# Transformer block: fill matmuls in column-tiled form beside the attention, and layer-norm transposes on TensorE

## The chip, the cores and the metric

One core of one Trainium2 chip. The metric is the device time in microseconds of one execution of the whole kernel. The kernel before was run three times: 1266.35, 1267.56 and 1269.32 us, median 1267.56.

The engines are called by their names in the profile: PE (TensorE matmul), PEld (its weight loads), DVE (VectorE), ACT (ScalarE), POOL (GpSimd), SP (the queue that issues the DMAs). PE computes `lhsT.T @ rhs`: lhsT is loaded as weights, rhs streams through, and the result lies in one of eight PSUM banks of 128 x 512 f32.

## The reference

A pre-norm transformer block in bf16 on one sequence of S = 2048 tokens, D = 1024, 32 heads of 32, a feed-forward width of F = 3584.

```
qkv = layernorm(x) @ wqkv                     # per head: q, k, v of 32 columns
p   = softmax(q @ k.T * 32**-0.5)             # 2048 x 2048 for each of 32 heads
h   = x + concat(p @ v) @ wo
out = h + gelu(layernorm(h) @ w1 + b1) @ w2 + b2
```

## The kernel before

**Planner.** The kernel is written down by a small planner in Python. Every operation is handed to `plan.task` with the buffers that it reads and writes and a cost in ns; the planner keeps for each engine the time at which it is free by these costs, works out the semaphore waits, and the order in which operations are recorded is the order in which each engine runs them. The chip knows nothing of the costs; they only decide the order. `pe` (L277) records a matmul, of kind F (128x128), R (32x128, a quarter of the rows) or C (128x32, a quarter of the columns); where the kind changes it books 105 ns more.

**Prologue (to about 69 us).** Sixteen tiles of 128 tokens of x are loaded, normalized (DVE statistics L456 to L458, POOL and DVE for the reciprocal root, ACT subtracts the mean L693, DVE scales L696) and transposed into `xnT`, since all projections need the model dimension on the partitions. Tiles 0 to 5 (`TP = 6`) are transposed on PE, eight 128x128 blocks a tile (L499), and evicted by ACT (L710). Tiles 6 to 15 are transposed by ten DMAs that SP issues (`ln1_t`, L714). A list of candidates with priorities (L732 to L763) interleaves these with the key projection of the first group of four heads for all four blocks of tokens (`proj_k`, L552), its queries (`proj_q`), a part of the values (`proj_v`, L590, two groups of 256 columns in one bank), and the bound on the scores of a group: the largest squared norm of queries and keys (`sumsq` L612, then `spread` L623).

**Attention (69 to 1129 us).** The queries are taken in four chunks of 512. Within a chunk the heads go by pairs, 16 of them; a pair has 32 score tiles of 128 keys x 512 queries, which make 11 units: ten of three PSUM banks and one of two. A unit is one group of score matmuls (`qk`, L937; three 32x128 matmuls that use different rows of PE at once), one exponential of ACT over its banks (L956), into one of six buffers `PT`. Scores of unit u use banks 0 to 2 or 3 to 5 by turns, so unit u + 2 waits for the exponential of unit u. For each key tile four value matmuls of 128x32 follow (`pv`, L970, L985): two heads, with V and with a column of ones for the sum, each in its own 32 columns of PE, all in bank 6. At the end of a pair DVE copies bank 6 out, and after two pairs it normalizes (L998 to L1015).

Before a pair starts, `qk_prereq` (L924) makes sure by `until` that the norms of its keys and queries are recorded: what is missing of them is recorded there and then, between two units.

**Fill.** All other matmuls run between the units, in bank 7: in the first chunk the remaining projections and norms (`fill0`, L788), in chunk c the output projection, the feed-forward layer and the late queries (`ffn`, L1104) of chunk c - 1. `group` (L510) is eight matmuls into one bank with an eviction by DVE (L561, L582, L1149, L1247); the second feed-forward matmul (L1280) is 28 into one bank. GELU is made of DVE operations and one tanh on ACT (L1256). The loop at L1338 chooses at every step among the next score group, value matmuls and a piece of fill, by what is ready in the planner's time; a quota spreads the fill over the chunk's units.

**Tail (1129 to 1266 us).** The output projection and the feed-forward layer of the last chunk, with transposes on PE, over all banks.

Of the kernel before, what the change touches and what calls it, by code (L numbers as in the profile page):

```python
# [13 lines left out]
P = 128  # L14
# [187 lines left out]
def build_kernel(nc, A_x, A_wqkv, A_wo, B_w1, B_b1, B_w2, B_b2, out):  # L202
    _, S, D = A_x.shape
    F = B_w1.shape[1]
# [3 lines left out]
    DC = D // P  # L208
    G = DC
    NP = 2 * G  # L210
    FC = F // P
# [62 lines left out]

    work = [0.0]

    def pe(fn, reads=(), writes=(), inc=True, cost=0.0, kind="F"):  # L277
        if kind == "F":
            work[0] += cost
        if mode[0] != kind:  # L280
            cost += 105.0
            mode[0] = kind
        plan.task(E.PE, fn, reads=reads, writes=writes, inc=inc, cost=cost)

    def mm(n):
        return n / 2.4 + 2.5


    base = (nc.sbuf_base + 63) // 64 * 64
# [92 lines left out]
    ps = T(nc.psum_tensor("ps", [P, 8, 512], dt.float32))  # L382
    B_ps = nbufs(8)
    OD = 6
# [125 lines left out]
    def group(mms, evac, reads_of, n=512, chunk=2, chs=()):  # L510
        bank = fbanks.next()
        k = len(mms)
        for i, (lhsT, rhs) in enumerate(mms):
            if i % chunk == 0:
                rd = []
                for j in range(i, min(k, i + chunk)):
                    rd += reads_of(j)
                yield Need(rd, [B_ps[bank]] if i == 0 else [], [c_ for c_ in chs if c_ is not None] if i == 0 else ())
            pe(lambda p, i=i, lhsT=lhsT, rhs=rhs: p.matmul(ps[:, bank, 0:n], lhsT, rhs, start=(i == 0), stop=(i == k - 1)),  # L519
               reads=reads_of(i), writes=[B_ps[bank]] if i in (0, k - 1) else [], inc=(i == k - 1), cost=mm(n))  # L520
            if i == k - 1:
                evac(bank)

# [66 lines left out]
    def proj_v(tt, q, eng="dve"):  # L590

        bank = fbanks.next()
        c0 = (q % 2) * 256
        for u in range(2):
            tc, o = (tt + u) // 4, ((tt + u) % 4) * P
            for dc in range(DC):
                if dc % 4 == 0:
                    yield Need(B_wv + [B_xnTf[tt + u]], [B_ps[bank]] if u == 0 and dc == 0 else [])
                pe(lambda p, u=u, tc=tc, o=o, dc=dc: p.matmul(ps[:, bank, u * 256:(u + 1) * 256], xnT[tc][:, dc, o:o + P], wv[:, dc, c0:c0 + 256],  # L599
                                                              start=(dc == 0), stop=(dc == DC - 1)),  # L600
                   reads=B_wv + [B_xnTf[tt + u]], writes=[B_ps[bank]] if dc in (0, DC - 1) else [], inc=(dc == DC - 1), cost=mm(256))
        o_ap = V[:, tt:tt + 2, q * 256:(q + 1) * 256]
        i_ap = ps[:, bank, :].rearrange("p (u c) -> p u c", u=2)
        B_o = [B_V[tt][q], B_V[tt + 1][q]]
        if eng == "act":
            act(lambda a: a.activation(o_ap, i_ap, ACT.Copy), reads=[B_ps[bank]], writes=B_o, cost=600)
        else:
            dve(lambda v: v.tensor_copy(o_ap, i_ap), reads=[B_ps[bank]], writes=B_o, cost=690)
        marks.add(("v", tt, q))
        marks.add(("v", tt + 1, q))  # L610
# [88 lines left out]
                       ("call", lambda tt=tt: ln1_t(tt), [B_x], [B_xnTf[tt]], 0)], True)  # L699
        chain(st + rs[:1] + [("call", spawn, [], [], 0)] + rs[1:] + [("call", lambda: marks.add(("rs", k)), [], [], 0)])  # L700

    TP = 6
    normed = set()

    def ln1_tp(tt):
# [43 lines left out]
    while ("kn", 0) not in marks or ("qn", 0, 0) not in marks:  # L749
# [10 lines left out]
        i = min(opts)[2]  # L760
# [176 lines left out]
    def qk(u):  # L937
        ci, p_, un = units[u]
        w = CH[ci][1]
        g, tc = p_ // 2, CH[ci][0] // 512  # L940
        s0 = 3 * (u % 2)
        s = qdl[(ci, p_)]
        banks = sorted({b for _, _, b, _ in un})
        wr = [B_ps[s0 + b] for b in banks]
        n = len(un)
        for i, (kt, h, b, o) in enumerate(un):
            rg = h + 2 * (kt % 2)
            pe(lambda p, kt=kt, rg=rg, b=b, o=o: p.matmul(  # L948
                ps[:, s0 + b, o:o + w], K2[32 * rg:32 * rg + 32, p_, kt // 2, :], Qd[32 * rg:32 * rg + 32, s, 0:w],
                start=True, stop=True, tile_position=(32 * rg, 0), skip_group_check=True),  # L950
                reads=[B_Qd[s][0], B_Qd[s][1], B_K2h[p_][kt // 4][kt % 2]],
                writes=wr if i in (0, n - 1) else [], inc=(i == n - 1), cost=mm(w) if i % 3 == 0 else 4, kind="R")
        o_ = u % NPT
        nb = len(banks)
        wa = 512 if n != 2 or w == 512 else w
        act(lambda a: a.activation(PT[:, o_, 0:nb, 0:wa], ps[:, s0:s0 + nb, 0:wa], ACT.Exp, bias=biasm[:, g, tc:tc + 1], scale=SCALE),  # L956
            reads=wr + [B_bias[g][tc]], writes=[B_PT[o_]], cost=180 + 0.833 * nb * wa)
# [12 lines left out]
    def pv():  # L970
        e = pending.popleft()
        ci, p_, kt, a_, b_ = e
        w = CH[ci][1]
        pr = p_ % 2
        until(("v", kt, p_ // 4))
        rd = pv_reads(e)
        start, stop = kt == 0, kt == NT - 1
        cols = (0, 1, 2, 3) if pr == 0 else (2, 3, 0, 1)
        for i in range(4):
            h = i % 2  # L980
            uu, b, o = (a_, b_)[h]
            c0 = 32 * cols[i]
            lhsT = V[:, kt, p_ * 64 + 32 * h:p_ * 64 + 32 * h + 32] if i < 2 else ones32[:, :]
            edge = (start and i == 0) or (stop and i == 3)
            pe(lambda p, c0=c0, lhsT=lhsT, uu=uu, b=b, o=o: p.matmul(  # L985
                ps[c0:c0 + 32, OD, 0:w], lhsT, PT[:, uu % NPT, b, o:o + w], start=start, stop=stop,
                tile_position=(0, c0), skip_group_check=True),
                reads=rd, writes=[B_ps[OD]] if edge else [], inc=(i == 3), cost=mm(w) if i == 0 else 4, kind="C")
        if stop:
            finish_pair(ci, p_)  # L990

# [112 lines left out]
    def ffn(ci, tail):  # L1104
# [163 lines left out]
        for hf in range(2):  # L1268
            turns = []
            for d4 in range(4):  # L1270
                db = hf * 4 + d4
                s = w2s[db]
                bank = fbanks.next()
                for fc in range(FC):
                    if fc == 6:
                        load_w2(db + len(B_w2_) - 1)
                    if fc % 2 == 0:
                        yield Need([B_gT[fc], B_gT[fc + 1], B_w2_[s]], [B_ps[bank]] if fc == 0 else [],
                                   [g_ch[fc], g_ch[fc + 1]])
                    pe(lambda p, fc=fc, s=s, bank=bank: p.matmul(ps[:, bank, 0:w], w2[:, s, fc, :], gT[:, fc, 0:w],  # L1280
                                                                 start=(fc == 0), stop=(fc == FC - 1)),
                       reads=[B_gT[fc], B_w2_[s]], writes=[B_ps[bank]] if fc in (0, FC - 1) else [], inc=(fc == FC - 1), cost=mm(w))
# [52 lines left out]
    u = 0  # L1335
    ph = 0
    seg, nf = None, 0
    while u < NU or pending:  # L1338
        t = plan.free[E.PE]
        service(t)  # L1340
# [68 lines left out]
        if best == INF:  # L1409
            if pending:  # L1410
                pv()
                seg = "C"
            elif not do_fill():
                raise RuntimeError("stuck")
        elif best == q_r:
            qk(u)
            u += 1
            seg, nf = None, 0
        elif best == f_r:
            do_fill()  # L1420
            seg, nf = "F", 1
        else:
            pvs(npv)
            seg = "C"

    rings = [([7, 6], 0), ([0, 1, 2, 3, 4, 5], 0)]
    both = [state, dict(state, gens=deque([ffn(len(CH) - 1, True)]), need=None, gen=None)]
# [113 lines left out]
```

## Time and profile before

| what | value |
|---|---|
| median of three runs | 1267.56 us |
| the profiled execution | 1268.39 us, span 1266.2 us, mean granted clock 0.984 |
| PE matmuls in the span | 9408, busy 1194.1 us |
| score matmuls, L948 | 2048 of 32x128, 512 columns |
| value matmuls, L985 | 2048 with V and 2048 with ones, of 128x32, 512 columns |
| exponentials, L956 | 704, busy 996.6 us |
| PE transposes of x, L499 | 48 |
| DMA transposes of x, L261 | 10 |
| first exponential, last exponential's end | 69.1 us, 1128.6 us |

Matmuls are pipelined: a row's mean (383 to 389 ns for 512 columns) is the length of one from its first to its last step, and what counts for the rate is the distance between starts. Busy time is the union of such lengths. "Idle before" is the pause of the engine ahead of an instruction, with what ended it. The granted clock is the share of full speed at which PE ran.

### The profile page before, as it was taken

The page shows a single profiled execution, that of the slowest core. Times are in us where ns is not written, and L with a number is a line of the kernel's source. Part 1 is how long each engine was busy: PE and PEld are TensorE (multiplying, and loading weights), DVE is VectorE, ACT ScalarE, POOL GpSimd, SP SyncE. Part 2 cuts the span into 40 slices and gives each one's busy share as a digit, 9 for nine tenths or more (in the row PEclk, how much of TensorE's full clock was granted, in tenths as well). Part 3 has the DMA queues.
Part 4 walks back from the last instruction along what each step waited for, and adds up shares of the span by engine and source line. Part 5 has one row for each costly group of instructions (what it writes and reads, how often), then busy time and mean ns, then how long its engine had stood idle before and what let it go on. Part 6 is the DMA issues. An engine that isn't in the chain of part 4 may idle for free.

```text
span 1266.2 us, 22935 instructions
## 1 busy us (share of the span) xinstructions
PE 1194.1 (94%) x9408; PEld 422.8 (33%) x9408; DVE 634.2 (50%) x1177; ACT 1115.8 (88%) x908; POOL 36.2 (3%) x180
## 2 busy tenths in 40 slices
PE   5699899899899999999999999999999999987998
PEld 2434334343233333333223233333223223323444
DVE  6433443435455878222466885223578832236820
ACT  5489899799999999999999999999999999962831
POOL 3300000000010000000010000000100000000000
PEclk9899999999999999999999999999999999997999
DMA  7441210201522324353622352352322514332743
GB/s 235 85 99 45 72 34 5 48 22 47 138 63 63 92 72 117 76 113 76 171 51 77 91 135 53 76 133 64 76 71 78 132 38 107 94 116 65 187 100 92
DMA packets 298809, 111.08 MB, mean 88 GB/s; under 512 B 216273, under 2 KB 296145, under 8 KB 298705
## 3 DMA queue, kind: packets, MB, share of 16 engines
q1 hardware_dynamic: 298704, 109.62, 34.1%
q8 instruction: 74, 1.21, 0.4%
q14 instruction: 31, 0.25, 0.1%
HBM read 83.90 MB, written 4.19 MB: 70 GB/s over the span
## 4 chain that ended last, share of the span: by engine, by line
PE 80%; DVE 9%; ACT 6%; issue 4%; DMA 1%; POOL 0%; SPq 0%; DVEq 0%; ACTq 0%
PE ps L519 27%; PE ps L985 17%; PE ps L1280 16%; PE ps L948 15%; ACT PT L956 5%; PE ps L599 4%; DVE Rg L1005 1%; DVE xh L1247 1%; DVE QT L1015 1%; DVE Sg L998 1%; DVE Rg L1011 1%; DVE lnst L456 1%; DVE rcp L1008 0%; DMA xnTl<-xr 0%; PE ps L499 0%
## 5 line engine op out<-in xcount | busy, mean ns | idle before, releaser
L956 ACT ACTIVATE PT<-ps,biasm 128x1536 bf16<-128x1536 f32 (+1 forms) x704 | 996.6, 1532 | 25.8 <-PE ps L948 19.0
L985 PE MATMUL ps<-PT,V 128*32 128x512 bf16 x2048 | 284.4, 384 | 1.8 <-ACT PT L956 1.1
L948 PE MATMUL ps<-Qd,K 32*128 32x512 bf16 x2048 | 275.1, 386 | 11.0 <-ACT PT L956 10.0
L985 PE MATMUL ps<-PT,ones 128*32 128x512 bf16 x2048 | 284.5, 384 | 0.0
L519 PE MATMUL ps<-hnT,w 128*128 128x512 bf16 x672 | 174.5, 383 | 4.4 <-DVE xh L1247 4.2
L1280 PE MATMUL ps<-gT,w 128*128 128x512 bf16 x672 | 173.2, 382 | 0.2 <-DVE oT L1287 0.2
L948 PEld LDWEIGHTS ps<-Qd,K 32*128 32x128 bf16 x2048 | 68.2, 91 | 291.1 <-ACT PT L956 146.2
L985 PEld LDWEIGHTS ps<-PT,V 128*32 128x32 bf16 x2048 | 77.4, 95 | 136.8 <-issue 84.2
L998 DVE COPY Sg<-ps 128x512 f32<-128x512 f32 x64 | 44.3, 692 | 151.1 <-PE ps L985 151.1
L1247 DVE TENSOR_SCALAR xh<-ps,b1f 128x512 bf16<-128x512 f32 x84 | 63.0, 750 | 51.6 <-PE ps L519 51.5
L519 PEld LDWEIGHTS ps<-hnT,w 128*128 128x128 bf16 x672 | 52.4, 98 | 93.8 <-issue 37.6
L1280 PEld LDWEIGHTS ps<-gT,w 128*128 128x128 bf16 x672 | 52.5, 97 | 80.6 <-issue 33.9
L985 PEld LDWEIGHTS ps<-PT,ones 128*32 128x32 bf16 x2048 | 77.6, 95 | 0.1
L1287 DVE TENSOR_SCALAR oT<-ps,b2f 128x512 bf16<-128x512 f32 x24 | 18.0, 750 | 104.9 <-PE ps L1280 104.8
L519 PE MATMUL ps<-xnTe,wk 128*128 128x512 bf16 x256 | 65.8, 389 | 3.7 <-DVE kn L619 1.8
L1257 DVE SCALAR_TENSOR_TENSOR gT<-tm,xh 128x512 bf16<-128x512 bf16 x84 | 57.0, 684 | 4.7 <-ACT tm L1256 4.2
L1254 DVE SCALAR_TENSOR_TENSOR tm<-tm,xh 128x512 bf16<-128x512 bf16 x84 | 58.1, 691 | 2.5
L1256 ACT ACTIVATE tm<-tm 128x512 bf16<-128x512 bf16 x84 | 53.6, 647 | 3.5 <-DVE tm L1254 3.0
L519 PE MATMUL ps<-hnT,w_t 128*128 128x512 bf16 x224 | 50.7, 391 | 1.2 <-ACT hnT L1215 1.2
L1280 PE MATMUL ps<-gT,w_t 128*128 128x512 bf16 x224 | 48.7, 379 | 0.0
L561 DVE CAST kst<-ps 128x512 bf16<-128x512 f32 x28 | 19.3, 688 | 54.6 <-PE ps L519 51.2
L1005 DVE STREAM_TRANSPOSE Rg<-Sg 64x512 f32<-64x512 f32 x64 | 45.1, 705 | 1.7
(106 smaller groups left out, 875.8 us busy)
## 6 DMA issues: line engine op xcount, KB each, us to landing
w<-in_B_w_dram SPq DMA_DIRECT2D x42, 512.0 KB, 3.8
w<-in_B_w_dram SPq DMA_DIRECT2D x24, 896.0 KB, 5.5
Qd<-QT SPq DMA_DIRECT2D x128, 64.0 KB, 2.5
w_t<-in_B_w_dram SPq DMA_DIRECT2D x14, 512.0 KB, 4.3
w_t<-in_B_w_dram SPq DMA_DIRECT2D x8, 896.0 KB, 5.5
wk<-in_A_wqkv_dram SPq DMA_DIRECT2D x20, 256.0 KB, 3.7
xr<-in_A_x_dram SPq DMA_DIRECT2D x16, 256.0 KB, 5.0
K<-kst SPq DMA_DIRECT2D x128, 32.0 KB, 1.9
```

The costliest lines, as they stand in the source:

```text
L519: pe(lambda p, i=i, lhsT=lhsT, rhs=rhs: p.matmul(ps[:, bank, 0:n], lhsT, rhs, start=(i == 0), stop=(i == k - 1)), reads=reads_of(i), write ...
L599: pe(lambda p, u=u, tc=tc, o=o, dc=dc: p.matmul(ps[:, bank, u * 256:(u + 1) * 256], xnT[tc][:, dc, o:o + P], wv[:, dc, c0:c0 + 256], start ...
L948: pe(lambda p, kt=kt, rg=rg, b=b, o=o: p.matmul(ps[:, s0 + b, o:o + w], K2[32 * rg:32 * rg + 32, p_, kt // 2, :], Qd[32 * rg:32 * rg + 32, ...
L956: act(lambda a: a.activation(PT[:, o_, 0:nb, 0:wa], ps[:, s0:s0 + nb, 0:wa], ACT.Exp, bias=biasm[:, g, tc:tc + 1], scale=SCALE), reads=wr ...
L985: pe(lambda p, c0=c0, lhsT=lhsT, uu=uu, b=b, o=o: p.matmul(ps[c0:c0 + 32, OD, 0:w], lhsT, PT[:, uu % NPT, b, o:o + w], start=start, stop=stop,
L998: dve(lambda v: v.tensor_copy(Sg[:, pr, 0:w], ps[:, OD, 0:w]), reads=[B_ps[OD]], writes=[B_Sg[pr]], cost=690)
L1005: st.append((E.DVE, lambda v, lo=lo, k=k: v.transpose(Rg[lo:lo + 64, 0:w], Sg[lo:lo + 64, k, 0:w]), [B_Sg[k]], [B_Rg[k]], 60 + 1.04 * w))
L1247: dve(lambda v: v.tensor_scalar(xh[:, gs, 0:w], ps[:, bank, 0:w], b1f[:, fc:fc + 1], 0.5, ALU.add, ALU.mult), reads=[B_ps[bank], Bf_b1f], ...
L1254: st.append((E.DVE, lambda v: v.scalar_tensor_tensor(tm[:, gs, 0:w], tm[:, gs, 0:w], GB, xh[:, gs, 0:w], ALU.add, ALU.mult), [Bt, Bx], [Bt ...
L1256: st.append((E.Activation, lambda a: a.activation(tm[:, gs, 0:w], tm[:, gs, 0:w], ACT.Tanh, scale=GK), [Bt], [Bt], 180 + .75 * w))
L1257: st.append((E.DVE, lambda v: v.scalar_tensor_tensor(gT[:, fc, 0:w], tm[:, gs, 0:w], 1.0, xh[:, gs, 0:w], ALU.add, ALU.mult), [Bt, Bx], [B ...
L1280: pe(lambda p, fc=fc, s=s, bank=bank: p.matmul(ps[:, bank, 0:w], w2[:, s, fc, :], gT[:, fc, 0:w], start=(fc == 0), stop=(fc == FC - 1)), r ...
```

## The change

1. Every 128x128 matmul that is opened while the attention loop records (`narrow[0]`) is issued as four matmuls of 128x32, on four quarters of the weights' columns, with the same moving operand, into the four quarters of the bank's partitions. They are of kind C, like the value matmuls; the planner books the first at the full cost and the other three at nothing, and a change of kind only against scores and the wide ones. Prologue and tail stay wide. The score and value matmuls beyond the first of a group are booked at 0 instead of 4 ns.
2. `TP` is 16 instead of 6: all sixteen tiles of x are transposed on PE and evicted by ACT; `ln1_t` is no longer called.

```
     def pe(fn, reads=(), writes=(), inc=True, cost=0.0, kind="F", fill=False):
-        if kind == "F":
+        if kind == "F" or fill:
             work[0] += cost
...
+    def wide(bank, c0, n, lhsT, rhs, start, stop, reads, writes, inc):
+
+        if start:
+            opened[bank] = narrow[0]
+        if not opened[bank]:
+            pe(lambda p: p.matmul(ps[:, bank, c0:c0 + n], lhsT, rhs, start=start, stop=stop), reads=reads, writes=writes, inc=inc, cost=mm(n))
+            return
+        for c in range(4):
+            pe(lambda p, c=c: p.matmul(ps[32 * c:32 * c + 32, bank, c0:c0 + n], lhsT[:, 32 * c:32 * c + 32], rhs, start=start, stop=stop,
+                                       tile_position=(0, 32 * c), skip_group_check=True),
+               reads=reads, writes=writes if c in (0, 3) else [], inc=inc and c == 3, cost=mm(n) if c == 0 else 0, kind="C", fill=True)
...
-            pe(lambda p, i=i, lhsT=lhsT, rhs=rhs: p.matmul(ps[:, bank, 0:n], lhsT, rhs, start=(i == 0), stop=(i == k - 1)),
-               reads=reads_of(i), writes=[B_ps[bank]] if i in (0, k - 1) else [], inc=(i == k - 1), cost=mm(n))
+            wide(bank, 0, n, lhsT, rhs, i == 0, i == k - 1, reads_of(i), [B_ps[bank]] if i in (0, k - 1) else [], i == k - 1)
...
-    TP = 6
+    TP = 16
...
-                writes=wr if i in (0, n - 1) else [], inc=(i == n - 1), cost=mm(w) if i % 3 == 0 else 4, kind="R")
+                writes=wr if i in (0, n - 1) else [], inc=(i == n - 1), cost=mm(w) if i % 3 == 0 else 0, kind="R")
...
-                reads=rd, writes=[B_ps[OD]] if edge else [], inc=(i == 3), cost=mm(w) if i == 0 else 4, kind="C")
+                reads=rd, writes=[B_ps[OD]] if edge else [], inc=(i == 3), cost=mm(w) if i == 0 else 0, kind="C")
...
+    narrow[0] = True
     while u < NU or pending:
...
+    narrow[0] = False
```

The matmuls of `proj_v` and of the second feed-forward layer call `wide` in the same way.

More of the change, by code (lines that the diff above doesn't have):

```diff
@@ L275, in build_kernel, with pe @@
     work = [0.0]
-    def pe(fn, reads=(), writes=(), inc=True, cost=0.0, kind="F"):
-        if kind == "F":
+    def pe(fn, reads=(), writes=(), inc=True, cost=0.0, kind="F", fill=False):
+        if kind == "F" or fill:
             work[0] += cost
@@ L286, in mm @@
         return n / 2.4 + 2.5
+    narrow = [False]
+    opened = {}
+    def wide(bank, c0, n, lhsT, rhs, start, stop, reads, writes, inc):
[8 more added lines that the diff above has]
+               reads=reads, writes=writes if c in (0, 3) else [], inc=inc and c == 3, cost=mm(n) if c == 0 else 0, kind="C", fill=True)
     base = (nc.sbuf_base + 63) // 64 * 64
@@ L598, in proj_v @@
                     yield Need(B_wv + [B_xnTf[tt + u]], [B_ps[bank]] if u == 0 and dc == 0 else [])
-                pe(lambda p, u=u, tc=tc, o=o, dc=dc: p.matmul(ps[:, bank, u * 256:(u + 1) * 256], xnT[tc][:, dc, o:o + P], wv[:, dc, c0:c0 + 256],
-                                                              start=(dc == 0), stop=(dc == DC - 1)),
-                   reads=B_wv + [B_xnTf[tt + u]], writes=[B_ps[bank]] if dc in (0, DC - 1) else [], inc=(dc == DC - 1), cost=mm(256))
+                wide(bank, u * 256, 256, xnT[tc][:, dc, o:o + P], wv[:, dc, c0:c0 + 256], dc == 0, dc == DC - 1,
+                     B_wv + [B_xnTf[tt + u]], [B_ps[bank]] if dc in (0, DC - 1) else [], dc == DC - 1)
         o_ap = V[:, tt:tt + 2, q * 256:(q + 1) * 256]
@@ L1279, in ffn @@
                                    [g_ch[fc], g_ch[fc + 1]])
-                    pe(lambda p, fc=fc, s=s, bank=bank: p.matmul(ps[:, bank, 0:w], w2[:, s, fc, :], gT[:, fc, 0:w],
-                                                                 start=(fc == 0), stop=(fc == FC - 1)),
-                       reads=[B_gT[fc], B_w2_[s]], writes=[B_ps[bank]] if fc in (0, FC - 1) else [], inc=(fc == FC - 1), cost=mm(w))
+                    wide(bank, 0, w, w2[:, s, fc, :], gT[:, fc, 0:w], fc == 0, fc == FC - 1,
+                         [B_gT[fc], B_w2_[s]], [B_ps[bank]] if fc in (0, FC - 1) else [], fc == FC - 1)
                 if tail:
```

## The prediction

> **What bounds the kernel now.** I read the page's shares first, then the chain of work that ended last, then the windows by stage, then the timeline of single stretches. The profiled execution took 1268.39 us (span 1266.2 plus 2.2 around it), 0.07% above the median 1267.56; all sums are against 1268.39.
>
> ```profile
> PE 1194.1 (94%) x9408; PEld 422.8 (33%) x9408; DVE 634.2 (50%) x1177; ACT 1115.8 (88%) x908; POOL 36.2 (3%) x180
> ...
> PE 80%; DVE 9%; ACT 6%; issue 4%; DMA 1%; POOL 0%; SPq 0%; DVEq 0%; ACTq 0%
> ```
>
> TensorE carries 80% of the chain, but ScalarE is busy too, and a share is an average over stages. The windows (columns: stretch, its length, busy us and count of PE, PEld, DVE, ACT, POOL, then granted clock, DMA share, GB/s) cut the attention at each 176th exponential, that is by chunk of 512 queries. The first two:
>
> ```profile
> 69.10:334.50 265.40, 250.78 (x2277) 98.13 (x2279) 111.11 (x206) 247.61 (x176) 0.68 (x3) 1.00 0.21 53
> 334.50:599.90 265.40, 261.36 (x2106) 82.80 (x2102) 141.79 (x251) 261.71 (x205) 4.89 (x24) 0.99 0.36 87
> ```
>
> In every chunk both engines are nearly full, so what TensorE saves can be cashed only until ScalarE's own floor. The timeline (start, length, engine, line, operation, count) prices both; ScalarE first, then TensorE:
>
> ```profile
> 498.97 1.57 ACT L956 ACTIVATE PT<-ps,biasm 128x1536 bf16<-128x1536 f32 x1
> 500.40 0.66 ACT L1256 ACTIVATE tm<-tm 128x512 bf16<-128x512 bf16 x1
> 500.92 3.00 ACT L956 ACTIVATE PT<-ps,biasm 128x1536 bf16<-128x1536 f32 x2
> ```
>
> ```profile
> 500.00 1.04 PE L519 MATMUL ps<-hnT,w 128*128 128x512 bf16 x4
> 500.97 0.39 PE L948 MATMUL ps<-Qd,K 32*128 32x512 bf16 x3
> ...
> 501.52 0.38 PE L985 MATMUL ps<-PT,V 128*32 128x512 bf16 x2
> 501.53 0.38 PE L985 MATMUL ps<-PT,ones 128*32 128x512 bf16 x2
> 501.74 0.38 PE L985 MATMUL ps<-PT,V 128*32 128x512 bf16 x2
> 501.74 0.38 PE L985 MATMUL ps<-PT,ones 128*32 128x512 bf16 x2
> 502.06 1.04 PE L1280 MATMUL ps<-gT,w 128*128 128x512 bf16 x4
> ```
>
> Four value matmuls of 128x32 (two with V, two with ones) start together, and the next four 0.216 us later (501.52 to 501.74), the pace of one 128x128 matmul (500.00 to 500.97 is four steps and a switch: 4 x 0.216 + 0.105). Three score matmuls of 32x128 also cost one step. Each change among the three shapes adds 0.105 (501.74 to 502.06 is 0.32). ScalarE: an exponential holds it 1.43 (498.97 to 500.40; 1.423 as a median of the trace), the two-bank one 1.00, a tanh 0.52. Its floor is 160 x 1.423 + 16 x 0.997 = 243.6 us in the first chunk and, with 28 tanh, 258.2 in each other. Measured are 265.4, 265.4, 264.4, 264.3, so ScalarE loses 21.8, 7.2, 6.2 and 6.1.
>
> **Part 1, the shape.** I counted steps and switches in the order of instructions that both kernels build. Second chunk before: 176 score groups, 257 value groups, 564 fills, which is 215.4 us, and 394 switches, 41.4: 256.8. After: 176, 258, 576 quads (124.3 us) and 354 switches: 255.4. By chunk TensorE needs 245.8, 256.8, 257.6, 252.3 before and 243.5, 255.4, 255.2, 241.2 after; fills that lay behind now fit where they belong. In all 1588 switches become 1409, 179 x 0.105 = 18.8 us less. In the new order no fill of the attention is left wide, so the change does what it says; the switch that stays is score to rest and back, twice a unit.
>
> What of it is on the path? Chunks two and three already differ from four by 5 us of TensorE slack, and ScalarE loses 6 to 7 in all of them. So slack hardly buys time there: I take 0.5 us for each, 1.5 together; the ends are 0 and all that ScalarE loses, 19.5.
>
> The first chunk is different: three waits make 14.5 of its 21.8 us. The scores of a pair need the bound on its keys, and when the key projection is behind, the order forces it through between two score groups:
>
> ```profile
> 229.36 0.39 PE L948 MATMUL ps<-Qd,K 32*128 32x512 bf16 x2
> 229.68 1.90 PE L519 MATMUL ps<-xnTl,wk 128*128 128x512 bf16 x8
> 232.37 0.85 PE L616 MATMUL ps<-sqk,blk 128*32 128x512 bf16 x4 [0.78 <-DVE kst L561]
> 234.09 1.89 PE L519 MATMUL ps<-xnTe,wk 128*128 128x512 bf16 x8 [0.88 <-DVE kn L619]
> 237.39 0.23 PE L629 MATMUL ps<-dg,ones_pp 128*128 128x128 bf16 x1 [1.41 <-DVE dg L627]
> 237.60 0.60 PE L948 MATMUL ps<-Qd,K 32*128 32x512 bf16 x6
> ```
>
> Scores at 229.36 and 237.60: 8.24 us, and ScalarE stands 6.7. A like place at 129.25 takes 6.46 (5.1 to 5.3 lost), one at 298.43 takes 3.96 (2.4 lost): the loss is the interval less some 1.45. In the new order the sum of squares stands one score group earlier at the first two, so 0.32 (switch) + 7 x 0.216 + 1.79 (last fill to the spread, 235.60 to 237.39) + 0.21 = 3.83 remain: 2.4 lost each. At the third, two of the eight quads remain behind the score group: 0.32 + 0.22 + 1.79 + 0.21 = 2.54, 1.1 lost. Gain 2.9 + 4.3 + 1.3 = 8.5 us. Ends: none, if ScalarE running ahead of the plan meets the same wait elsewhere, and 14.5.
>
> Two prices have no row. A quad of 256 columns (384 of them, in the first chunk): a wide one steps in 0.109 (32 in 3.66 us at 51.72), and a 512-column quad in 0.216; I take 0.109, nearest in length, the other end is 384 x 0.107 = 41 us. And the pace of issue: a chunk now issues 3848 matmuls in 264 us (69 ns each), before some 2110 (125 ns). The densest run in the trace is 20 in 1.19 us, 60 ns. I take it as free, since TensorE's queue starts eight instructions within 11 ns (weights and matmuls of one quad, 501.291 to 501.302), and fetches its code in 16 KB pieces of 1 to 1.5 us, one per 7 us at the new pace against 11 at the densest now.
>
> **Part 2, the transposes.** Ten DMA transposes of 1.26 us each leave SP's queue (with the K copies behind them); TensorE gets 80 transposes, 0.107 each at half clock and 0.06 at full (16 in 1.06 us at 27.66), and ScalarE ten evictions of 1.02. Today the end of the prologue is:
>
> ```profile
> 59.87 3.57 PE L519 MATMUL ps<-xnTl,wk 128*128 128x512 bf16 x8 [4.50 <-issue]
> 63.24 2.94 PE L599 MATMUL ps<-wv,xnTl 128*128 128x256 bf16 x16
> ```
>
> The last key projection starts at 59.87, behind the DMA transposes of tiles 14 and 15 (issued from 55.63), and runs at half clock because TensorE stood for 4.5 us. Walking the new order: ScalarE is in order, and its evictions push the centring of the last two tiles from 47.9 to about 52.0; scaled at 55.1, transposed by 57.5, both evicted by about 59. So the projection starts hardly earlier, but without the pause it and the 16 behind it (6.2 us now) may run at full clock in 3.5. Gain 2.7 and the rest of the walk 0.8, less the chance of half clock: I take 3.0. Ends: 5 gained, 3 lost, if ScalarE's order makes the last tiles later. DMA traffic is no matter. The tail keeps its wide matmuls and its own transposes: 0.
>
> Sum: 8.5 + 1.5 + 3.0 = 13.0; 1268.4 - 13.0 = **1255.4 us**, 1.0% faster.
>
> **Rivals.** *Issue becomes the bound* (slower): the 2368 quads cost more than a wide matmul. Against it are the rows above; for it, no row has such a density over more than some 20 matmuls. Every 10 ns on a quad are 23.7 us, of which the slack of ScalarE's floor over TensorE (0, 3, 3, 17 us) takes up to 23, and the 13 gained come on top: from about 15 ns a quad (0.231 instead of 0.216) it is slower. At twice that, 30 ns, 71 us less 23 less 13: 1303 us. The Trainium skill, TensorE: Matmul & The Clock Gate, section "Wait — 56ns, not 53.3ns?", says that with hardware decode off the sequencer's code spends about 62 ns on each matmul. By that rule a quad would take 248 ns of either width, 1984 x 32 + 384 x 139 ns = 117 us more, and the time, as an estimate, would be about 1268 + 117 - 23 - 13 = 1349; the eight starts within 11 ns speak against it, though the trace holds that pace for one quad alone. The rival's chance, by the rows: 0.15, with the 256-column price in it.
> *The prologue loses* what it should gain (3 lost): 1261, still faster; 0.12.
> *Nothing moves* (0.08): the forced waits reappear, as keys still come just at their deadline, and the rest is ScalarE's: 1266 to 1269.
> *The coupling loosens* (0.12): half of the 19.5 us goes too: 1247.
> *As forecast*: 0.53.
>
> Faster by over 0.2% (about what a measurement tells from no change) 0.77, within 0.2% 0.08, slower 0.15. The range reaches from the loosened coupling with 5 us of prologue, 1244, to 1275, a quad some 18 ns dearer.
>
> **What would show it.** Right: quads 0.216 apart in the attention; switches of 0.32 only beside scores; ScalarE's waits near 130 and 230 us at 2 to 3 us; first exponential near 66; chunks two to four at 263 to 265 each. Wrong: quads over 0.230 apart or TensorE waiting on "issue"; the first exponential later than 69; ScalarE's loss unchanged in the first chunk.

## The result: 0.76% slower, and the profile after

The changed kernel takes **1277.84 us** (median of 4 runs, 1277.76 to 1278.62) against 1268.44 (4 runs of the kernel before): a ratio of 1.0076, 95% interval [1.0058, 1.0094]. The forecast was 1255.4 us, a gain. The profiled execution took 1277.87 us (span 1275.7) and is compared with the 1268.39 us of before.

The page of the changed kernel, the lines that answer to those of before and the group of the exponentials (the code lines have moved: L948 is now L962, L956 L970, L985 L999; L300 issues the quads, four 128x32 matmuls that stand for one wide one, and L297 the wide ones that are left):

```profile
PE 1194.3 (94%) x16576; PEld 456.3 (36%) x16592; DVE 634.0 (50%) x1177; ACT 1130.3 (89%) x918; POOL 36.2 (3%) x180
...
PE 74%; DVE 12%; ACT 7%; issue 5%; DMA 1%; POOL 1%; SPq 0%; DVEq 0%; ACTq 0%; POOLq 0%
...
L970 ACT ACTIVATE PT<-ps,biasm 128x1536 bf16<-128x1536 f32 (+1 forms) x704 | 1000.0, 1515 | 33.6 <-PE ps L962 28.6
```

PE issues 7168 matmuls more and is busy as long as before, to 0.2 us; its share of the chain falls from 80 to 74%. What the span grew by lies in PE's pauses, 81.4 us instead of 72.1 (span less busy time). The windows of the changed kernel, cut at each 176th exponential as before (stretch, length, busy us and count of PE, PEld, DVE, ACT, POOL, granted clock, DMA share, GB/s; the last row is the tail):

```profile
63.73:323.86 260.13, 249.21 (x4398) 105.74 (x4386) 111.19 (x206) 248.08 (x176) 0.68 (x3) 1.00 0.23 56
323.86:596.68 272.82, 263.17 (x3850) 90.92 (x3850) 143.79 (x256) 264.14 (x205) 4.74 (x24) 0.99 0.35 87
596.68:867.88 271.20, 264.23 (x3858) 90.75 (x3850) 142.26 (x252) 263.67 (x205) 4.68 (x24) 0.99 0.37 92
867.88:1137.53 269.65, 253.54 (x3589) 83.67 (x3581) 133.79 (x237) 261.91 (x205) 5.56 (x24) 0.96 0.32 83
1137.53:1275.65 138.12, 121.31 (x572) 55.61 (x580) 66.34 (x134) 50.10 (x81) 0.00 (x0) 0.92 0.44 116
```

| stretch | before, us | after, us | difference | forecast |
|---|---|---|---|---|
| to the first exponential | 69.1 | 63.7 | -5.4 | -3.0 |
| first chunk | 265.4 | 260.1 | -5.3 | -8.5 |
| chunks two, three, four | 265.4, 264.4, 264.3 | 272.8, 271.2, 269.6 | +7.4, +6.8, +5.3 | -0.5 each |
| tail | 137.6 | 138.1 | +0.5 | 0 |

The first two lines gave together 10.7 us where 11.5 were forecast; the sum is near because one gain was forecast too small and the other too large. Chunks two to four took back 19.5. In them ScalarE's loss against its floor (exponentials and tanh, worked out as in the prediction) rose from 19.5 to 39.0 us.

**Who waits there.** The views of waits over chunks two to four (engine, line, what it waited for, us in total, times, longest) say it from ScalarE's side, first the kernel before, then the changed one:

```profile
ACT PT L956 <- PE ps L948: 4.7, 13, 0.9
```

```profile
ACT PT L970 <- PE ps L962: 17.3, 35, 2.4
```

and from PE's side, in the same order:

```profile
PE ps L948 <- ACT PT L956: 7.5, 15, 0.8
PE ps L519 <- DVE xh L1247: 4.2, 13, 0.7
```

```profile
PE ps L962 <- ACT PT L970: 14.6, 29, 0.8
PE ps L300 <- DVE xh L1261: 9.0, 21, 0.9
PE ps L999 <- DVE Sg L1012: 3.8, 4, 3.1
```

Both engines wait more, and for each other: in some places ScalarE waits for scores (12.6 us more of it, out of the 19.5), in others PE for ScalarE. That speaks for work lying in the wrong places and not for one engine that has become slower. The timeline of the changed kernel at a place of the first sort (start, length, engine, line, operation, count):

```profile
445.13 0.39 PE L962 MATMUL ps<-Qd,K 32*128 32x512 bf16 x3
445.45 0.39 PE L999 MATMUL ps<-PT,V 128*32 128x512 bf16 x2
445.46 0.39 PE L999 MATMUL ps<-PT,ones 128*32 128x512 bf16 x2
445.68 1.90 PE L300 MATMUL ps<-hnT,w 128*32 128x512 bf16 x32
447.51 0.39 PE L962 MATMUL ps<-Qd,K 32*128 32x512 bf16 x3
```

Eight quads between two score groups that lie 2.38 us apart, where an exponential takes 1.42. And of the second sort, at the start of the fourth chunk:

```profile
869.54 0.39 PE L962 MATMUL ps<-Qd,K 32*128 32x512 bf16 x3 [0.71 <-ACT PT L970]
872.99 0.61 PE L999 MATMUL ps<-PT,V 128*32 128x512 bf16 x2 [3.06 <-DVE Sg L1012]
873.00 0.61 PE L999 MATMUL ps<-PT,ones 128*32 128x512 bf16 x2
873.54 0.61 PE L962 MATMUL ps<-Qd,K 32*128 32x512 bf16 x3
```

PE has no fill left (the last lies at 865.4, the next at 876.0), stands for 3.06 us, and a matmul is 0.61 us long afterwards instead of 0.38. The windows of the stretches at half clock in the chunks of the changed kernel (the 0.50 is the granted clock; the last one goes on for 2.8 us in the tail):

```profile
327.90:331.30 3.40, 2.96 (x27) 0.88 (x27) 1.76 (x3) 3.24 (x3) 0.00 (x0) 0.50 0.74 180
594.20:604.40 10.20, 9.30 (x69) 2.03 (x69) 4.68 (x8) 9.81 (x8) 0.00 (x0) 0.50 0.92 259
870.60:877.40 6.80, 4.41 (x38) 1.07 (x38) 6.02 (x12) 4.80 (x4) 0.00 (x0) 0.50 0.57 181
911.60:921.80 10.20, 9.22 (x69) 2.01 (x69) 1.30 (x4) 7.76 (x6) 0.54 (x3) 0.50 0.29 66
1133.50:1137.50 4.00, 3.58 (x25) 0.60 (x25) 0.00 (x0) 4.00 (x4) 0.00 (x0) 0.50 0.86 273
```

Together 34.6 us; before it was 10.2 (3.4 and 6.8). Each lies in or just behind a stretch without fill. Such stretches of over 4.5 us at the ends and starts of chunks are 5.9, 6.2, 11.1 and 7.1 us long before, and 6.5, 13.8, 10.6, 14.0 and 9.9 after. The Trainium skill, TensorE: Matmul & The Clock Gate, section "What's actually happening", has the clock set from an activity window of some 3.4 us; the whole lengths of 3.4, 6.8 and 10.2 us agree.

**Theory.** The order was at fault, not the shape: the fill is packed too early, ScalarE starves there, and later PE runs dry. What made the order is the smallest edit of the change, score and value matmuls beyond the first booked at 0 instead of 4 ns. The loop records a score group once `q_r`, the end of the exponential that holds its banks *by the plan*, is at most 60 ns ahead of PE's plan, and until then it records fill that is ready:

```
        if q_r <= t + 60:
            qk(u)
...
            if f_r <= t + 60:
                do_fill()
```

So PE is given as much work between two score groups as the plan thinks an exponential lasts. It books 180 + 0.833 x 1536 = 1459.5 ns; the trace has 1423. Before, PE was booked too long as well: 2 x 4 ns a score group and 1024 value groups / 704 units x 12 ns, 25 ns a unit. The surplus of work over ScalarE's real pace was 36 - 25 = **11 ns** a unit; the change made it **36**. **Rivals:** the quads themselves cost something that their pace doesn't show (code, weight loads); the transposes on PE upset what follows; or every order is a draw of its own.

### The profile page after: what moved, and what is told of

Its sections match the earlier page's. It is cut to its first block, busy times and chain, and to the rows that moved or that the text cites. A ratio compares the mean times of both kernels' runs of the same rounds, so it can differ in the third digit from the quotient of the medians.

```text
span 1275.7 us, 37274 instructions
## 1 busy us (share of the span) xinstructions
PE 1194.3 (94%) x16576; PEld 456.3 (36%) x16592; DVE 634.0 (50%) x1177; ACT 1130.3 (89%) x918; POOL 36.2 (3%) x180
## 3 DMA queue, kind: packets, MB, share of 16 engines
q8 instruction: 130, 2.13, 0.7%
## 4 chain that ended last, share of the span: by engine, by line
PE 74%; DVE 12%; ACT 7%; issue 5%; DMA 1%; POOL 1%; SPq 0%; DVEq 0%; ACTq 0%; POOLq 0%
PE ps L300 35%; PE ps L999 15%; PE ps L962 14%; PE ps L297 10%; ACT PT L970 5%; DVE Rg L1019 2%; DVE xh L1261 2%; DVE lnst L472 1%; DVE QT L1029 1%; DVE Sg L1012 1%; DVE Rg L1025 1%; DVE rcp L1022 0%; DVE kst L576 0%; DVE QT L597 0%; PE ps L515 0%
## 5 line engine op out<-in xcount | busy, mean ns | idle before, releaser
L970 ACT ACTIVATE PT<-ps,biasm 128x1536 bf16<-128x1536 f32 (+1 forms) x704 | 1000.0, 1515 | 33.6 <-PE ps L962 28.6
L999 PE MATMUL ps<-PT,V 128*32 128x512 bf16 x2048 | 299.9, 387 | 4.3 <-DVE Sg L1012 4.2
L999 PE MATMUL ps<-PT,ones 128*32 128x512 bf16 x2048 | 300.2, 387 | 0.0
L962 PE MATMUL ps<-Qd,K 32*128 32x512 bf16 x2048 | 277.8, 389 | 17.2 <-ACT PT L970 16.2
L300 PE MATMUL ps<-hnT,w 128*32 128x512 bf16 x2688 | 177.3, 384 | 10.7 <-DVE xh L1261 7.8
L300 PE MATMUL ps<-gT,w 128*32 128x512 bf16 x2688 | 180.3, 382 | 1.4 <-DVE xh L1261 1.2
L962 PEld LDWEIGHTS ps<-Qd,K 32*128 32x128 bf16 x2048 | 68.3, 91 | 305.8 <-issue 175.1
L999 PEld LDWEIGHTS ps<-PT,V 128*32 128x32 bf16 x2048 | 86.3, 96 | 110.5 <-issue 59.2
L999 PEld LDWEIGHTS ps<-PT,ones 128*32 128x32 bf16 x2048 | 86.4, 96 | 18.0
L300 PEld LDWEIGHTS ps<-hnT,w 128*32 128x32 bf16 x2688 | 60.9, 96 | 87.4 <-issue 36.9
L300 PEld LDWEIGHTS ps<-gT,w 128*32 128x32 bf16 x2688 | 55.7, 95 | 77.5 <-issue 34.7
L300 PE MATMUL ps<-xnTe,wk 128*32 128x512 bf16 x832 | 53.8, 381 | 1.6 <-DVE kn L633 0.9
L297 PE MATMUL ps<-hnT,w_t 128*128 128x512 bf16 x219 | 50.8, 393 | 1.6 <-ACT hnT L1229 1.2
L297 PE MATMUL ps<-gT,w_t 128*128 128x512 bf16 x219 | 48.4, 379 | 0.3
L1029 DVE TENSOR_TENSOR QT<-Sg,Rg 64x512 bf16<-64x512 f32 x64 | 43.9, 685 | 2.0
```

Of the source, the lines that this page charges most:

```text
L297: pe(lambda p: p.matmul(ps[:, bank, c0:c0 + n], lhsT, rhs, start=start, stop=stop), reads=reads, writes=writes, inc=inc, cost=mm(n))
L300: pe(lambda p, c=c: p.matmul(ps[32 * c:32 * c + 32, bank, c0:c0 + n], lhsT[:, 32 * c:32 * c + 32], rhs, start=start, stop=stop, tile_posit ...
L962: pe(lambda p, kt=kt, rg=rg, b=b, o=o: p.matmul(ps[:, s0 + b, o:o + w], K2[32 * rg:32 * rg + 32, p_, kt // 2, :], Qd[32 * rg:32 * rg + 32, ...
L999: pe(lambda p, c0=c0, lhsT=lhsT, uu=uu, b=b, o=o: p.matmul(ps[c0:c0 + 32, OD, 0:w], lhsT, PT[:, uu % NPT, b, o:o + w], start=start, stop=stop,
L1029: st.append((E.DVE, lambda v, lo=lo, k=k: v.tensor_tensor(QT[lo:lo + 64, QS[tc], g, o:o + w], Sg[lo:lo + 64, k, 0:w], Rg[lo:lo + 64, 0:w], ...
```

## The experiments

All ratios are against the kernel before on the same chip, with the 95% interval. Chunks, tails and waits are those of one profiled execution, which can lie up to 4 us from the median of its kernel.

**1. The transposes alone.**

```
-    TP = 6
+    TP = 16
```

> The kernel before with TP = 16 alone. Changed kernel: first exponential at 63.4 us instead of 69.1, and the whole is 9.4 us slower. If the transposes only help (theory: the loss is made in chunks two to four), the first exponential comes at 63 to 65 us, the rest keeps its length, and the time is 1261 to 1264. If the moved prologue upsets what follows (rival), it is 1266 or more.

Measured 1264.72 us, 0.9978 [0.9963, 0.9992]. First exponential at 64.5 us, chunks 265.1, 265.1, 265.2, 264.2. The first exponential comes 4.6 us earlier, 3.8 of which arrive at the end, and no chunk moves: this part is a gain and no suspect.

**2. The shape alone.** The order, the bookings and `TP = 6` of before; each wide matmul of the fill in the attention is issued as four inside one planned task (the part of the edit in `wide`).

```
+        def fn(p):
+            if not quad:
+                return p.matmul(ps[:, bank, c0:c0 + n], lhsT, rhs, start=start, stop=stop)
+            for c in range(4):
+                r = p.matmul(ps[32 * c:32 * c + 32, bank, c0:c0 + n], lhsT[:, 32 * c:32 * c + 32], rhs, start=start, stop=stop,
+                             tile_position=(0, 32 * c), skip_group_check=True)
+            return r
+
+        pe(fn, reads=reads, writes=writes, inc=inc, cost=mm(n))
```

> The order, the bookings and the prologue of the kernel before; in the attention each wide matmul is issued as a quad of 128x32. Theory (the new order loses, the quads are free): TensorE steps 0.216 a quad, the 196 switches between fill and values go (20 us of TensorE), chunks two to four take 262 to 265 us each, and the time is 1258 to 1266. Rival (quads cost the chip something that is not in their steps): chunks two to four at 268 to 273, as in the changed kernel, and 1272 or more.

1261.06 us, 0.9945 [0.9926, 0.9963]. Its second and third chunks in the windows:

```profile
332.10:594.52 262.42, 257.85 (x3810) 89.21 (x3806) 141.63 (x251) 260.68 (x204) 4.91 (x24) 1.00 0.36 89
594.52:858.18 263.66, 258.59 (x3801) 88.72 (x3795) 143.37 (x256) 260.98 (x205) 4.74 (x24) 0.99 0.38 97
```

Nearly as many matmuls as in the changed kernel (3810 against 3850 in the second chunk), and 262.4 us instead of 272.8. The quads are a gain of 7.5 us where the order is left alone.

**3. The order alone.** The changed kernel with its order, each quad issued as one wide matmul.

```
-        for c in range(4):
-            pe(lambda p, c=c: p.matmul(ps[32 * c:32 * c + 32, bank, c0:c0 + n], lhsT[:, 32 * c:32 * c + 32], rhs, start=start, stop=stop,
-                                       tile_position=(0, 32 * c), skip_group_check=True),
-               reads=reads, writes=writes if c in (0, 3) else [], inc=inc and c == 3, cost=mm(n) if c == 0 else 0, kind="C", fill=True)
+        pe(lambda p: p.matmul(ps[:, bank, c0:c0 + n], lhsT, rhs, start=start, stop=stop),
+           reads=reads, writes=writes, inc=inc, cost=mm(n), kind="C", fill=True)
```

> The changed kernel with its order and bookings, but each quad of the fill issued as one wide matmul. Theory (order): it stays slower than the kernel before, and pays the switches between fill and values again, which the order does not avoid: 1280 to 1300. Rival (quads): chunks two to four go back to 264 to 266, and the time is 1262 to 1268.

1289.36 us, 1.0176 [1.0150, 1.0202]. The same two chunks:

```profile
325.91:600.61 274.70, 265.56 (x2122) 82.89 (x2122) 143.79 (x256) 264.41 (x205) 4.73 (x24) 1.00 0.34 86
600.61:876.08 275.47, 269.85 (x2130) 82.33 (x2122) 142.20 (x252) 264.76 (x206) 4.68 (x24) 0.99 0.35 90
```

The loss comes without a single quad, and the quads make the new order better (1277.84) and not worse. With experiment 2, the rival that quads cost something hidden is out. The 20.8 us here are not the price of the order alone: this plan doesn't book the changes of kind between wide fill and value matmuls, and the trace has 306 of them against 199 before, some 11 us of PE at 0.105 each, by estimate.

**4. 4 ns for every further matmul**, those of the fill's quads too.

```
-               reads=reads, writes=writes if c in (0, 3) else [], inc=inc and c == 3, cost=mm(n) if c == 0 else 0, kind="C", fill=True)
+               reads=reads, writes=writes if c in (0, 3) else [], inc=inc and c == 3, cost=mm(n) if c == 0 else 4, kind="C", fill=True)
...
-                writes=wr if i in (0, n - 1) else [], inc=(i == n - 1), cost=mm(w) if i % 3 == 0 else 0, kind="R")
+                writes=wr if i in (0, n - 1) else [], inc=(i == n - 1), cost=mm(w) if i % 3 == 0 else 4, kind="R")
...
-                reads=rd, writes=[B_ps[OD]] if edge else [], inc=(i == 3), cost=mm(w) if i == 0 else 0, kind="C")
+                reads=rd, writes=[B_ps[OD]] if edge else [], inc=(i == 3), cost=mm(w) if i == 0 else 4, kind="C")
```

> The changed kernel with the second and further matmuls of a group booked at 4 ns again, the three further ones of a quad too. If the zero booking spoils the order (the old 4 ns left some 26 ns of slack a unit on TensorE), most of the loss goes: 1262 to 1270. If it is the missing price of a switch between fill and values, or something else, it stays at 1274 to 1281.

1274.95 us, 1.0054 [1.0035, 1.0073]. The time lies in the expectation's second range, although its first reading was right on the chunks: two to four come back to 263.2, 266.1, 263.4, but the first is 271.0 and the tail 145.3 us. Now PE is booked too long against ScalarE (2368 quads / 704 units x 12 ns add 40), the plan puts fill off, and 106 pieces of it (84 wide matmuls and 22 quads) are left over to the tail. So the chunks also come back because they hold less work, and an error of the booking in the other direction is paid in another place.

**5. The small edit alone, in the kernel before.** No quad, six PE transposes.

```
-                writes=wr if i in (0, n - 1) else [], inc=(i == n - 1), cost=mm(w) if i % 3 == 0 else 4, kind="R")
+                writes=wr if i in (0, n - 1) else [], inc=(i == n - 1), cost=mm(w) if i % 3 == 0 else 0, kind="R")
...
-                reads=rd, writes=[B_ps[OD]] if edge else [], inc=(i == 3), cost=mm(w) if i == 0 else 4, kind="C")
+                reads=rd, writes=[B_ps[OD]] if edge else [], inc=(i == 3), cost=mm(w) if i == 0 else 0, kind="C")
```

> The kernel before, wide matmuls and TP = 6, with the further score and value matmuls of a group booked at 0 instead of 4 ns. Theory (the 4 ns, 8 a score group and 12 a value quad, some 25 ns a unit, stand for what the exponential is booked too long, 1.46 against 1.42 us measured, and without them the order puts more fill into a unit than ScalarE waits for): chunks two to four grow from 264 to 270 or so each, as in the changed kernel, and the time is 1280 to 1292. Rival (the booking matters only where fill and values share a kind): 1264 to 1272.

1280.12 us, 1.0087 [1.0062, 1.0113]: 11.3 us from two numbers that the chip never sees. Chunks two to four: 269.2, 268.4, 268.8.

**6. Experiments 1 and 2 together** (shape and transposes, order and bookings as before).

> Both gains without the new bookings: quads in the order of the kernel before, and TP = 16. If the two add up (-7.4 and -3.8 measured alone): 1256 to 1259, which is about what was forecast for the change. If they overlap: 1260 to 1264.

1257.68 us, 0.9917 [0.9900, 0.9934]. This is about what the prediction had in mind; the two parts add up (3.8 and 7.5 alone, 11.1 together).

**7. 4 ns for score and value matmuls only**, in the changed kernel (the last two edits of experiment 4).

> The changed kernel with 4 ns again for the further score and value matmuls; the three further ones of a fill quad stay at 0, so the fill is booked at its pace and the tail gets nothing left over. If the missing 4 ns are the whole loss: chunks two to four at 263 to 266, first chunk near 260, 1255 to 1262. If the missing switch between fill and values spoils the order by itself: 1266 to 1278.

1271.65 us (10 runs, 1267.94 to 1276.01), 1.0027 [1.0010, 1.0043]: in the expectation's second range. Chunks two to four 267.2, 268.7, 265.7: 12 of the 19.5 us return there in the profiled execution, the fastest of the ten, while the first takes 263.6 instead of 260.1. So the missing 4 ns are not the whole loss. With the old order (experiments 2 and 6) the plan has more in hand: it books 105 ns for each of some 203 changes between fill and value matmuls, which quads don't need. The next run shows that these bookings need not come back.

**8. ScalarE booked as measured**, the zeros of the change kept.

```
-            reads=wr + [B_bias[g][tc]], writes=[B_PT[o_]], cost=180 + 0.833 * nb * wa)
+            reads=wr + [B_bias[g][tc]], writes=[B_PT[o_]], cost=143 + 0.833 * nb * wa)
...
-                    st.append((E.Activation, lambda a: a.activation(tm[:, gs, 0:w], tm[:, gs, 0:w], ACT.Tanh, scale=GK), [Bt], [Bt], 180 + .75 * w))
+                    st.append((E.Activation, lambda a: a.activation(tm[:, gs, 0:w], tm[:, gs, 0:w], ACT.Tanh, scale=GK), [Bt], [Bt], 136 + .75 * w))
```

> The changed kernel with the exponential and the tanh booked at what the trace shows (1.42 and 0.52 us instead of 1.46 and 0.56), all else as changed, the zero booking too. If the loss comes from a plan that takes ScalarE to be slower than it is: chunks two to four at 262 to 266 and 1255 to 1264. If it does not matter what ScalarE is booked at: 1274 to 1280.

**1255.85 us, 0.9893 [0.9872, 0.9914]**, the lowest median here (its interval overlaps that of experiment 6): 22 us less than the changed kernel, by two numbers of the plan. Its chunks:

```profile
64.46:323.83 259.37, 249.48 (x4401) 106.77 (x4389) 111.43 (x206) 246.85 (x177) 0.77 (x3) 1.00 0.23 56
323.83:585.70 261.87, 257.51 (x3805) 88.79 (x3807) 141.82 (x251) 260.48 (x205) 4.77 (x24) 1.00 0.36 89
585.70:849.25 263.55, 258.78 (x3834) 89.59 (x3829) 143.33 (x256) 260.78 (x206) 4.89 (x24) 1.00 0.39 98
849.25:1113.46 264.21, 253.30 (x3657) 84.51 (x3647) 134.60 (x238) 261.05 (x205) 4.73 (x24) 0.98 0.32 81
```

and its view of waits over chunks two to four, against 17.3 and 9.0 us in the changed kernel:

```profile
ACT PT L970 <- PE ps L962: 6.8, 17, 1.1
```

```profile
PE ps L300 <- DVE xh L1261: 4.7, 15, 0.5
```

The stretches without fill are down to 5.2, 6.2, 13.7 and 8.7 us, and ScalarE's loss in these chunks is 15.0 us.

**9. The same correction in experiment 5's kernel** (wide matmuls).

> The kernel before (wide matmuls, six PE transposes) with the further score and value matmuls booked at 0, which alone cost 11 us, and now with the exponential booked 37 ns and the tanh of the fill 44 ns shorter, as measured. Theory (the bookings of PE and of ScalarE have to agree; too long an exponential lets the plan put more fill between two score groups than the real one covers): chunks two to four come back from 269 to 262 to 265 us each; the built order leaves 44 fills over to the tail, which grows by 3 to 5 us; in all 1262 to 1270. Rival (the cure worked only because the fills are quads): chunks stay at 267 to 270 and the time near 1280 or above it with the longer tail.

1263.55 us, 0.9961 [0.9945, 0.9976]: chunks two to four 261.6, 262.4, 265.0, tail 139.0 us. The time and the chunks are about what the theory said, only the tail grew by 1.4 against the kernel before and not by 3 to 5. Chunks two to four hold 39 fills less than in experiment 5, 8.4 us of PE at 0.216; the whole time, 16.6 us less, counts that work in the tail. So the cure is not bound to quads.

**10. ScalarE booked longer still** (exponential 217 instead of 180, tanh 224), in the changed kernel.

> The changed kernel with the exponential booked 37 ns and the tanh of the fill 44 ns longer than in it, twice as far from the measured durations. Theory: the plan believes ScalarE to be slower still, packs more fill beside each exponential, the fill runs out sooner, PE idles more at each chunk's end and falls to half clock: chunks two to four at 274 to 282 us each, in all 1288 to 1305. Rival (the gain of the shorter booking was a lucky order and not a trend): 1270 to 1285, chunks as in the changed kernel.

1285.00 us, 1.0136 [1.0120, 1.0152]: at the upper edge of the rival's range, 3 us short of the theory's. Chunks two and three are about as the theory had them (276.4 and 273.6 against 274 to 282), the fourth isn't (268.5). By itself this run tells a direction, not a law; the next one decides. The first two stretches without fill grow from 6.5 and 13.8 to 11.2 and 24.0 us; the other three are a little shorter than in the changed kernel (10.1, 12.1 and 9.7). The clock in its second and third chunks:

```profile
327.94:604.34 276.40, 268.26 (x3854) 91.38 (x3850) 143.46 (x256) 264.47 (x206) 4.76 (x24) 0.96 0.36 91
604.34:877.98 273.64, 264.71 (x3858) 90.50 (x3854) 143.63 (x256) 263.81 (x206) 4.74 (x24) 0.98 0.34 83
```

**11. Half way** (exponential 161, tanh 158).

> The changed kernel with the exponential booked at 161 ns and 0.833 ns for each column, and the tanh at 158, half way between the changed kernel (180: 1277.8 us) and the one booked as measured (143 and 136: 1255.9 us). Theory (a trend): between the two, 1262 to 1272, chunks two to four at 264 to 269 us each. Rival (each order is a draw of its own and the booking has no trend): outside that, under 1258 or over 1275.

1268.46 us, 0.9997 [0.9986, 1.0008], chunks two to four 267.3, 267.1, 267.4. The rival is out. With 143, 161, 180 and 217 the time is 1255.9, 1268.5, 1277.8 and 1285.0: a trend and no draw, though not a straight line.

**12. ScalarE as measured in experiment 6's kernel.**

> Quads issued in the order that the 4 ns bookings give, all sixteen tiles transposed on PE (1257.7 us without more), and now with ScalarE booked as measured. Theory: the 4 ns and the short exponential together book PE too long against ScalarE, so fill is put off: 56 fills are left over to the tail, which grows by 4 to 6 us, while chunks two to four gain 1 to 2 us each for what they have lost in work: 1256 to 1261. Rival (a booking nearer to the measured durations is better in every case): the tail stays and the chunks gain, 1250 to 1255.

1266.26 us, 0.9984 [0.9975, 0.9994]: 8.6 us *slower* than experiment 6, more than the theory's 1256 to 1261, and its rival is refuted outright. Chunks two to four gain 2.3 us in sum (261.6, 261.0, 263.5; the fourth loses 1.3), with 50 fills left over to the tail. The tail is 142.1 us as expected, but the first chunk takes 270.4, as in experiment 4 (271.0). ScalarE's timeline in its first chunk, the three places with waits of over 2 us:

```profile
132.09 37.89 ACT L974 ACTIVATE PT<-ps,biasm 128x1536 bf16<-128x1536 f32 x27 [5.96 <-PE ps L966]
234.54 1.54 ACT L974 ACTIVATE PT<-ps,biasm 128x1536 bf16<-128x1536 f32 x1 [10.11 <-PE ps L966]
302.87 15.43 ACT L974 ACTIVATE PT<-ps,biasm 128x1536 bf16<-128x1536 f32 x11 [6.59 <-PE ps L966]
```

These are the forced waits of the prediction's first chunk. At the second and the third place the trace has one group of the key projection more (32 matmuls of 128x32) between the two score groups than experiment 6; at the first it is 64 matmuls of the value projection. The fill that was put off is forced through there. The waits are 22.7 us here, 4.28, 6.76 and 2.19 in experiment 6 (13.2 together), 6.61, 9.72 and 5.64 in experiment 4, and 6.4 together in the changed kernel. In experiment 8 they are 9.7, and its first chunk is the shortest of all (259.4): putting fill off is paid here, packing it ahead in chunks two to four, and that booking pays little of either.

**All in one table.** Surplus: booked exponential less 1423, less what PE is booked too long a unit (25 by the 4 ns of scores and values, 40 by those of the quads, 203 x 105 / 704 = 30 where the plan books changes that quads don't make), in ns.

| kernel | surplus | chunks two to four, us | first chunk | tail | median |
|---|---|---|---|---|---|
| 4: all at 4 ns | -29 | 792.6 | 271.0 | 145.3 | 1274.95 |
| 12: experiment 6, ScalarE as measured | -55 | 786.1 | 270.4 | 142.1 | 1266.26 |
| 6: quads, old order, 16 PE transposes | -19 | 788.4 | 264.5 | 136.1 | 1257.68 |
| 8: ScalarE as measured | 0 | 789.6 | 259.4 | 136.3 | 1255.85 |
| 9: wide, ScalarE as measured | 0 | 789.0 | 266.0 | 139.0 | 1263.55 |
| before | 11 | 794.1 | 265.4 | 137.6 | 1268.4 |
| 7: 4 ns for scores and values | 11 | 801.7 | 263.6 | 136.4 | 1271.65 |
| 11: half way | 18 | 801.8 | 261.1 | 138.1 | 1268.46 |
| 5: wide, booked at 0 | 36 | 806.5 | 266.2 | 137.8 | 1280.12 |
| changed kernel | 36 | 813.7 | 260.1 | 138.1 | 1277.84 |
| 10: booked longer | 73 | 818.6 | 263.3 | 138.0 | 1285.00 |

From 0 on, the chunks grow with the surplus. Below zero they gain little or nothing more, though in experiments 4 and 12 they hold 106 and 50 fills less, and there the first chunk and the tail pay. The surplus isn't all: at 11 and at 36 the chunks of the kernel with quads are some 7 us longer than those of the wide one, and no run says why. The surplus leaves the tanh out. Experiments 1 and 2 are left out, as their bookings are those of before and of 6, and experiment 3, whose wide matmuls need changes that its plan didn't book.

## Why the prediction was wrong, step by step

- **Chunks two to four: the step that failed.** "So slack hardly buys time there: I take 0.5 us for each, 1.5 together; the ends are 0 and all that ScalarE loses, 19.5." They lost 19.5; that the two figures are equal is chance. The ends lay on the side of a gain only, and by the sums PE needs 1.4 to 11.1 us less in each chunk. But a sum over a chunk holds only if the work lies where it can be hidden, and the order had moved: 570, 562 and 536 fills in chunks two to four before, 578, 578 and 512 after, in the traces. That was read as "fills that lay behind now fit where they belong"; it was the plan packing beyond ScalarE's pace.
- **An edit that got no price.** The prediction costs quads, switches and transposes, but not the change from 4 to 0 ns. It is 25 ns x 176 = 4.5 us of PE's plan in each chunk; experiment 5 gives 11.3 us for it. The two numbers that showed its sign were both at hand: 1459.5 ns booked and 1423 measured, for the same exponential.
- **The forced waits of the first chunk: right.** The view of the timeline that answers to 229.36 to 237.60:

```profile
223.18 0.39 PE L962 MATMUL ps<-Qd,K 32*128 32x512 bf16 x2
223.71 1.91 PE L300 MATMUL ps<-xnTe,wk 128*32 128x512 bf16 x32
227.04 0.23 PE L643 MATMUL ps<-dg,ones_pp 128*128 128x128 bf16 x1 [1.42 <-DVE dg L641]
227.25 0.60 PE L962 MATMUL ps<-Qd,K 32*128 32x512 bf16 x6
```

  Scores 4.07 us apart instead of 8.24 (forecast 3.83). ScalarE's waits at the three places are 2.85, 2.38 and 1.20 us (forecast 2.4, 2.4 and 1.1), 7.8 us less than before. The chunk gained 5.3: 2.5 us are lost elsewhere in it, one wait of 1.16 at 105.4 among them. This is a gain of the order and not of the shape: with quads in the old order (experiment 2) the first chunk takes 264.1 us, with wide matmuls in the new one (experiment 3) 261.9.
- **The prologue: right, the size too small.** 5.4 instead of 3.0 us. The cause named is there, the last projections run at full clock in 3.4 us, and they also begin 1.9 us earlier, which the walk had called "hardly earlier":

```profile
57.99 1.67 PE L297 MATMUL ps<-xnTl,wk 128*128 128x512 bf16 x7 [1.81 <-ACT xnTl L724]
59.50 1.91 PE L297 MATMUL ps<-wv,xnTl 128*128 128x256 bf16 x16
```

- **Quads at the wide pace and free issue: right.** Quads of 512 columns are 0.216 us apart (median of 1467 pairs of fill quads), those of 256 columns 0.109 (336). The rival that issue becomes the bound is refuted:

```profile
118.34 1.05 PE L300 MATMUL ps<-wv,xnTl 128*32 128x256 bf16 x32
119.32 0.39 PE L962 MATMUL ps<-Qd,K 32*128 32x512 bf16 x3
```

  0.98 us less one change of 0.105 is 27.3 ns for each of 32 matmuls; the densest run before had 60. The Trainium skill, TensorE: Matmul & The Clock Gate, section "Wait — 56ns, not 53.3ns?", has two floors for a matmul, about 25 ns and, with hardware decode off, about 62. The 62 isn't seen here; the mean of 27.3 lies above the 25, but the four matmuls of a quad start mostly 2 to 5 ns apart, so that the 25 doesn't hold between them. The changes of 0.32 us stand beside scores, as forecast: of 1409 changes 17 are elsewhere, before 204.
- **Rivals.** None of them was what happened. The one on the slower side was made of the shape, and "the coupling loosens" knew only one direction.

What stays open: how the 19.5 us divide. The stretches without fill are 24.5 us longer; where they run at full clock PE is busy 15.3 of 24.6 us, so some 9 us of its time are left unused, by this estimate. Half clock (24.4 us more) and the fill that is packed too closely between scores are what is left for the rest. The three are coupled, and no run took one away and left the others.

## What to carry to other kernels

In a kernel whose order comes from a planner, every booked cost is part of the program: price a change of 4 ns by its count, and against the error of the engine that it is balanced with. Two wrong bookings may cancel; before one is put right, compare both with the trace (here 1459.5 booked, 1423 measured) and correct them together, since an error on either side is paid, in starved exponentials or in fill left over. Where two engines are both nearly full, look at the order and not at the sum: what is moved forward, and what lies where the moved work is missing later.

## Not expected of the hardware

- Four matmuls of 128x32 in place of one of 128x128 cost nothing that these traces show: steps of 0.216 and 0.109 us at 512 and 256 columns as before, down to 27.3 ns for each matmul over 32 in a row.
- The instruction queue fetched 130 packets and 2.13 MB instead of 74 and 1.21, and no wait is seen from it: of the changed kernel's pauses of PE, the three put down to issue (1.17 us the longest) all lie outside the attention.
- In a stage where PE is busy 94% of the time (253.54 of 269.65 us), two stretches of 10.6 and 14.0 us with scores and value matmuls alone were enough for 6.8 and 10.2 us of half clock, which reached into the fill that followed: at 876.0 us 16 matmuls of 128x32 took 1.76 us, the next 16 at 878.0 took 1.05. Idle PE costs once more when the work comes back.
